# Loads taken apart and moved ahead, and a multiply put off, in a one-core training step of two linear-attention and two gated layers

## The chip, the cores and the metric

The kernel runs on one core of a Trainium2 chip. The metric is the device time of one execution in microseconds (us); smaller is better. The kernel before takes 1132.42 us, the median of three runs (1132.08 to 1135.51 us). The profiled execution, which all lines of the profile below come from, has a span of 1134.6 us.

## The reference

`x` has 2048 rows of 512 bf16 values. Four layers are applied, A, B, A, B, each to the layer norm of `x` and added to `x`; the two A layers share their weights, and so do the two B layers. The kernel returns the output and the gradients of `x` and of all five weights for a given `grad_out`.

```python
def _A_ref(x, wqkv, wo):              # linear attention, 32 heads of 16
    q, k, v = split_heads(x @ wqkv)
    phi = lambda t: jnp.where(t > 0, t + 1, jnp.exp(t)) + 1e-6
    pq, pk = phi(q), phi(k)
    kv = einsum("bhsd,bhse->bhde", pk, v);  z = einsum("bhsd->bhd", pk)
    o = einsum("bhqd,bhde->bhqe", pq, kv) / (einsum("bhqd,bhd->bhq", pq, z)[..., None] + 1e-6)
    return merge_heads(o) @ wo

def _B_ref(x, w_gate, w_up, w_down):  # 512 -> 1376 -> 512
    return (_sigmoid(x @ w_gate) * (x @ w_up)) @ w_down

x = x + _A_ref(_layernorm(x), wqkv, wo);  x = x + _B_ref(_layernorm(x), w_gate, w_up, w_down)
x = x + _A_ref(_layernorm(x), wqkv, wo);  x = x + _B_ref(_layernorm(x), w_gate, w_up, w_down)
# returned: x, and the gradients of sum(x * grad_out)
```

## The kernel before

Rows are handled in 4 blocks of 512 (`NBLK`), a block in 4 tiles of 128 rows, and the 1376 columns of a B layer in 11 chunks `fc` of 128. The layers are numbered 0 to 3. In order of time the program runs: layer 0 (A) to about 74 us, layer 1 (`b_fwd`, with the second half of layer 0 between its chunks) to about 250 us, layer 2 (A), then `b_both`, which does layer 3 forward and backward at once, to about 525 us; then backward through layer 2 (`a_bwd`, to 642 us), layer 1 (`b_bwd`, to 767 us) and layer 0 (`a_bwd`, to about 888 us); and last the weight gradients, the tail, to the end. A scheduler orders the instructions of each engine; each engine then works through its own list. The queue of SyncE (SP) issues most transfers, in the order of its list.

In the code, `...` marks what is cut, and L numbers are the lines that the profile names. The gated chunk, used in `b_fwd` and `b_both`. `hh` is the hidden value, `sd` holds the two factors that the backward pass needs:

```python
def glu(k, hT, fc):
    mm4(k, g_ps[:], ...wg...);  mm4(k, u_ps[:], ...wu...)          # 4 + 4 matmuls
    nc.scalar.activation(g_ps[:], g_ps[:], ACT.Tanh, scale=-0.5)   # L647
    nc.scalar.activation(sd[:, 0, :], g_ps[:], ACT.Identity, bias=k.onef[:], scale=-1.0)           # L648
    nc.vector.scalar_tensor_tensor(hh[:], sd[:, 0, :], 0.5, u_ps[:], ALU.mult, ALU.mult)           # L649
    nc.scalar.activation(sd[:, 1, :], g_ps[:], ACT.Identity, bias=k.onef[:])                       # L650
    nc.gpsimd.tensor_tensor(sd[:, 1, :], sd[:, 1, :], hh[:], ALU.mult)                             # L651
```

In `b_fwd`, `down(b)` multiplies the hidden values by `w_down`, adds to `x`, and asks at once for the layer norm of the next layer (`nxt.need`). In `b_both` each chunk ends with a multiply on VectorE:

```python
            hh, dd = glu(k, ln.hT[b], fc)
            mm4(k, ps[:], ...wdT..., ...gTs...)                    # dhh_ps
            nc.scalar.mul(dhh[:], ps[:], 0.5)                      # L732
            k.last_mul = nc.vector.tensor_tensor(dd, dhh..., dd, ALU.mult)     # L733
```

`k.last_mul` also holds back the transposing loads of the two weights that `b_both`'s own backward half (`dh_b`, L790) needs; a small memset on GpSimd follows the second of them:

```python
def load_b_bwd(k, t, nm, first):
    held(k, first, nc.sync.dma_start_transpose(out=t[:, 0:NFC - 1, :], in_=k.w_in[nm][:, 0:(NFC - 1) * P]))  # L418
    nc.sync.dma_start_transpose(out=t[:, NFC - 1, :], in_=k.w_in[nm][:, F - P:F])                            # L419
    nc.gpsimd.memset(t[0:FDUP, NFC - 1, :], 0.0)                                                             # L420
```

Backward through an A layer, first half. `qr` holds two saved arrays of a block, `qp` and `rp`, and the pool `p_sh` has two buffers:

```python
    for b in range(NBLK):
        qr = k.p_sh.tile([P, 2, NDC, SB], BF16, name="qr_l", tag="sh")
        qp, rp = qr[:, 0], qr[:, 1]
        nc.sync.dma_start(out=flat(qr), in_=sv["qr"][b])                       # L991, 1024 KB
        nc.sync.dma_start(out=flat(qn), in_=sv["qn"][b])
        dqT = p_dq.tile([P, NDC, SB], BF16, name="dqT_t")                      # 4 buffers
        for dc in range(NDC):
            mm4(k, ps[:], ...MT..., ...gT...)                                  # dq_ps
            k.mark = nc.scalar.copy(dq[:], ps[:])                              # L1005, dq_sb, 3 buffers
            nc.vector.tensor_tensor(u_t[:], dq[:], qp[:, dc, :], ALU.mult)     # L1007
            # two steps later, soft():
            nc.tensor.matmul(t_ps[:], lhsT=k.bdmask[:], rhs=u_t[:], ...)       # L977
            nc.vector.scalar_tensor_tensor(w_t[:], t_ps[:], nz, dq[:], ...)    # L979
            nc.gpsimd.tensor_tensor(dqT[:, dc, :], w_t[:], rp[:, dc, :], ALU.mult)   # L980
            nc.vector.scalar_tensor_tensor(u_t[:], t_ps[:], -1.0, qp[:, dc, :], ...) # L981
```

The tail. A gradient of 512 columns takes one pass over 16 row tiles for each of two layers; `pieces` loads the turned operand by transposing transfers into the pool `dw_set_end` (6 buffers of 512 rows), `load_all` the row operand (2 MB), and `put` takes a finished bank out of PSUM:

```python
        k.p_set, k.p_dst = pool("dw_set_end", 6), pool("dw_stage_end", 6)
        for i, a in ((0, 1), (1, 0), (1, 1), (2, 0), (2, 1)):
            if (i, a) == (2, 0):
                g1 = load_all(...)                 # into a pool of its own
            joint(i, a)                            # w_up, w_gate: L1199
        for i, s in enumerate(SETS):
            dw_rows(k, "wd", s, [(g1, sv[1]["hhT"])], sv[3]["wd"])     # w_down: L1217
            if i == 0:   h2 = load_all(...)
            elif i == 1: h0 = load_all(...)
        for i, nm in ((1, "dkT"), (0, "dqT")):     # w_qkv: L1199
            dw_cols(...)
            if i: dw_small(k)                      # L1148, L1153

def put(...):  k.nc.scalar.copy(new[0:r, 0:w], ps);  ...dma_start(out=..., in_=new)     # L1126
```

Of the kernel before, what the change touches and what calls it, by code (L numbers as in the profile page):

```python
# [16 lines left out]
D = 512  # L17
# [3 lines left out]
P = 128  # L21
# [612 lines left out]

def glu(k, hT, fc):

    nc = k.nc
    g_ps = k.ps.tile([P, SB], F32, name="g_ps", tag="bank")
    mm4(k, g_ps[:], lambda c: k.wg[:, c, FC0[fc]:FC0[fc] + P], lambda c: hT[:, :, c, :])
    u_ps = k.ps.tile([P, SB], F32, name="u_ps", tag="bank")  # L640
    mm4(k, u_ps[:], lambda c: k.wu[:, c, FC0[fc]:FC0[fc] + P], lambda c: hT[:, :, c, :])
    hh = k.p_hh.tile([P, SB], BF16, name="hh_t")
    if k.n_sd % 2 == 0:
        k.sd2 = k.p_sd.tile([P, 2, 2, SB], BF16, name="sd_t", tag="sd")
    sd = k.sd2[:, k.n_sd % 2]
    k.n_sd += 1
    nc.scalar.activation(g_ps[:], g_ps[:], ACT.Tanh, scale=-0.5)  # L647
    nc.scalar.activation(sd[:, 0, :], g_ps[:], ACT.Identity, bias=k.onef[:], scale=-1.0)  # L648
    nc.vector.scalar_tensor_tensor(hh[:], sd[:, 0, :], 0.5, u_ps[:], ALU.mult, ALU.mult)  # L649
    nc.scalar.activation(sd[:, 1, :], g_ps[:], ACT.Identity, bias=k.onef[:])  # L650
    nc.gpsimd.tensor_tensor(sd[:, 1, :], sd[:, 1, :], hh[:], ALU.mult)  # L651
    return hh, sd
# [7 lines left out]
def b_fwd(k, l, ln, nxt):  # L660
# [9 lines left out]
    def down(b):  # L670
        ys = [k.ps.tile([P, D], F32, name="y_ps", tag="bank") for _ in range(NB)]
        for fcs in (range(NFC - 1), (NFC - 1,)):
            for j in range(NB):
                for fc in fcs:
                    nc.tensor.matmul(ys[j][:], lhsT=hhs[b][fc][:, rows(j)], rhs=k.wd[:, fc, :],
                                     start=(fc == 0), stop=(fc == NFC - 1))
        for j in range(NB):
            add_x(k, b * NB + j, ys[j])
        nxt.need(b * NB + NB - 1)

    for b in range(NBLK):
# [3 lines left out]
        for fc in range(NFC):  # L685
            hh, sd = glu(k, ln.hT[b], fc)
            hhs[b].append(hh)
            if late:
                store()
            late.append((b, fc, hh, sd))  # L690
            yield b, fc
    store()
    down(NBLK - 1)


# [8 lines left out]
def b_both(k, l, ln, ctx):  # L704
# [6 lines left out]
    def down(b):  # L711
        for j in range(NB):
# [6 lines left out]
            if j % 2:  # L719
                k.st.dma_start(out=by_tile(k.out0, st - 1, 2), in_=ost[:])  # L720

    for b in range(NBLK):
        ln.need(b * NB + NB - 1)
# [3 lines left out]
        for fc in range(NFC):  # L727
# [4 lines left out]
            nc.scalar.mul(dhh[:], ps[:], 0.5)  # L732
            k.last_mul = nc.vector.tensor_tensor(dd, dhh[:].unsqueeze(1).to_broadcast([P, 2, SB]), dd, ALU.mult)  # L733
            hhs[b].append(hh)
            dds[b].append(dd)
            if b:
                turn_dd(k, sv, b, fc, dd)
            else:
                store_dd(k, sv, b, fc, dd, nc.sync)
            store_hh(k, sv, b, fc, hh, k.st)  # L740
# [7 lines left out]
            if b == NBLK - 1 and fc == 5:  # L748
                k.early = a_grads(k, 0)
            yield b, fc  # L750
    b = NBLK - 1
    down(b)
# [45 lines left out]
def backward(k):  # L798
    nc, tc = k.nc, k.tc
    with ExitStack() as ctx:  # L800
# [19 lines left out]
        k.fill.step(NFC * NST)  # L820
        h3, h1 = load_all(k, sv[3]["h"], "h_all"), load_all(k, sv[1]["h"], "h_all")
        joint = lambda i, a: dw_cols(k, ("wu", "wg")[a], 0, SETS[i],
                                     [(h3, sv[3]["ddT"][a], sv[3]["ddN"][:, :, :, a]), (h1, sv[1]["ddT"][a])])
        k.p_dst = mpool("dw_stage", 6)
        joint(0, 0)
        mctx.close()
        k.p_set, k.p_dst = pool("dw_set_end", 6), pool("dw_stage_end", 6)
        k.p_sm = pool("dw_small", 2)
        p_all, p_end = k.p_all, pool("dw_all_end", 2)
        for i, a in ((0, 1), (1, 0), (1, 1), (2, 0), (2, 1)):  # L830
            if (i, a) == (2, 0):
                k.p_all = p_end
                g1 = load_all(k, sv[1]["g"], "g_all")
                k.p_all = p_all
            joint(i, a)
        for i, s in enumerate(SETS):
            dw_rows(k, "wd", s, [(g1, sv[1]["hhT"])], sv[3]["wd"])
            if i == 0:
                h2 = load_all(k, sv[2]["h"], "h_all")
            elif i == 1:  # L840
                h0 = load_all(k, sv[0]["h"], "h_all")
        for i, nm in ((1, "dkT"), (0, "dqT")):
# [118 lines left out]
def a_bwd1(k, l, big, ph1, p_dq):  # L961
# [4 lines left out]
    CT_ps = [k.ps2.tile([P, D], F32, name="CT_ps", tag="dwbank") for _ in range(NDC)]  # L966
    late, gs, dqTs = [], [k.early], []

# [5 lines left out]

    def soft(b, dc, dq, u_t, qp, rp, dqT):
        t_ps = k.ps.tile([P, SB], F32, name="t_ps", tag="bank")
        nc.tensor.matmul(t_ps[:], lhsT=k.bdmask[:], rhs=u_t[:], start=True, stop=True)  # L977
        w_t = ph1.tile([P, SB], BF16, name="w_t")
        nc.vector.scalar_tensor_tensor(w_t[:], t_ps[:], A["nz"][:, dc:dc + 1], dq[:], ALU.mult, ALU.add)  # L979
        nc.gpsimd.tensor_tensor(dqT[:, dc, :], w_t[:], rp[:, dc, :], ALU.mult)  # L980
        nc.vector.scalar_tensor_tensor(u_t[:], t_ps[:], -1.0, qp[:, dc, :], ALU.mult, ALU.mult,  # L981
                                       accum_out=dzp[:, dc, b:b + 1])
        if dc == NDC - 1:
            k.st.dma_start(out=by_chunk(sv["dqT"], b), in_=dqT[:])

    k.fill.step(12)
    for b in range(NBLK):
        g_t, gT = gs[b]
        qr = k.p_sh.tile([P, 2, NDC, SB], BF16, name="qr_l", tag="sh")
        qp, rp = qr[:, 0], qr[:, 1]  # L990
        nc.sync.dma_start(out=flat(qr), in_=sv["qr"][b])  # L991
        qn = k.p_h.tile([P, NDC, NB, P], BF16, name="qn_l", tag="h_t")
        nc.sync.dma_start(out=flat(qn), in_=sv["qn"][b])
        if b == 1 and l == 2:
            nc.sync.dma_start_transpose(out=k.woT[:], in_=k.w_in["wo"])
            nc.sync.dma_start_transpose(out=k.wqkvT[:], in_=k.w_in["wqkv"])
        if b == NBLK - 1 and l == 2:
            held(k, k.mark, nc.sync.dma_start_transpose(out=k.wdT[:], in_=k.w_in["wd"]))
        dqT = p_dq.tile([P, NDC, SB], BF16, name="dqT_t")
        dqTs.append(dqT)  # L1000
        for dc in range(NDC):
# [5 lines left out]
            nc.vector.tensor_tensor(u_t[:], dq[:], qp[:, dc, :], ALU.mult)  # L1007
            late.append((b, dc, dq, u_t, qp, rp, dqT))
            k.fill.step(2)
            if len(late) > 2:  # L1010
                soft(*late.pop(0))
            if dc in (0, 2) and b + 1 < NBLK:
                g = a_grads(k, b + 1, dc // 2)
                if dc:
                    gs.append(g)
        sums(b, g_t, qn)
    while late:
# [104 lines left out]
def put(k, ps, nm, rs, cs, eng=None):  # L1122

    r, w = ps.shape[0], ps.shape[1]
    new = k.p_dst.tile([P, D], BF16, name="dw_new")
    k.nc.scalar.copy(new[0:r, 0:w], ps)  # L1126
    (eng or k.st).dma_start(out=k.outs[nm][rs, cs], in_=new[0:r, 0:w])  # L1127
# [29 lines left out]

def load_all(k, src, name):
    t = k.p_all.tile([P, NST, D], BF16, name=name, tag="all")
    for b in range(NBLK):  # L1160
        k.nc.sync.dma_start(out=t[:, b * NB:(b + 1) * NB, :], in_=by_tile(src, b * NB, NB))
    return t


def pieces(k, nat, src, c0, w, turned=None):

    for b in range(NBLK):
        if len(nat.shape) == 2:
            n = k.p_set.tile([P, NB, D], BF16, name="nat_t", tag="set_t")
            k.nc.sync.dma_start(out=n[:], in_=by_tile(nat, b * NB, NB))  # L1170
        t = k.p_set.tile([P, NB, w], BF16, name="set_t", tag="set_t")
# [4 lines left out]
        for j in range(NB):  # L1176
            st = b * NB + j
            yield st, (n[:, j, :] if len(nat.shape) == 2 else nat[:, st, :]), t[:, j, :]

# [75 lines left out]
```

## Time and profile before

| What | Value |
|---|---|
| Time, median of three runs | 1132.42 us |
| Span of the profiled execution | 1134.6 us |
| TensorE (PE) busy | 1074.8 us |
| VectorE (DVE) busy | 529.1 us |
| ScalarE (ACT) busy | 487.7 us |
| GpSimd (POOL) busy | 324.5 us |
| Moved by DMA | 248.12 MB, 219 GB/s in the mean |

How to read it: the busy times say how full an engine is over the whole span, not what it waited for. The list of waits names, for each engine, the line that stood idle and whose end released it, with the total, the number of times and the longest. The view by stretches of time gives the busy time of each engine in a stretch, the clock that TensorE was granted (1.00 is full), and the share of the 16 DMA engines in use (it can come out a little above 1). The timeline lists instructions in order, with the idle time before each in brackets. A matmul of 512 columns is shown as 379 ns long, but they overlap: the timeline has 11 of them starting every 2.37 us, so one occupies TensorE for 0.216 us.

### The profile page before, as it was taken

How to read it: one execution, taken by the hardware profiler on the slowest of the kernel's cores; microseconds unless marked ns; L12 is line 12 of the kernel's file. 1: busy time of each engine (PE TensorE's matmuls, PEld its weight loads, DVE VectorE, ACT ScalarE, POOL GpSimd, SP SyncE). 2: the span in 40 equal slices, each digit the busy share in tenths (PEclk: the TensorE clock that was granted, in tenths of full speed). 3: DMA queues.
4: the chain of work that ended last, by engine and by line, in shares of the span. 5: the costliest groups of instructions: out<-in, count | busy, mean ns of one | idle time of the engine just before them, and what ended most of it. 6: DMA issues, size and time to landing. Idle time of an engine off the chain costs nothing.

```text
span 1134.6 us, 15573 instructions
## 1 busy us (share of the span) xinstructions
PE 1074.8 (95%) x5529; PEld 509.6 (45%) x5624; DVE 529.1 (47%) x983; ACT 487.7 (43%) x1002; POOL 324.5 (29%) x427
## 2 busy tenths in 40 slices
PE   6989999998899999999899999999799999999898
PEld 3444444444334444444444444444344444464343
DVE  7685765667734445434657634546667100000100
ACT  3476977547635546453434533336236200000011
POOL 5425645303632625141433200003523200001110
PEclk9999999999999999999999999999999999999999
DMA  8977888679993939399996798759982797699995
GB/s 260 263 229 241 249 244 242 192 180 240 281 231 84 251 81 247 80 253 274 221 342 163 218 274 235 230 186 285 322 223 85 177 280 176 149 179 238 276 232 134
DMA packets 376557, 248.12 MB, mean 219 GB/s; under 512 B 288784, under 2 KB 341040, under 8 KB 374688
## 3 DMA queue, kind: packets, MB, share of 16 engines
q1 hardware_dynamic: 361424, 197.73, 70.0%
q0 software_dynamic: 15056, 49.39, 13.1%
q8 instruction: 44, 0.72, 0.3%
q14 instruction: 33, 0.27, 0.1%
HBM read 74.48 MB, written 102.20 MB: 156 GB/s over the span
## 4 chain that ended last, share of the span: by engine, by line
PE 26%; issue 20%; POOL 4%; DMA 3%; DVE 2%; ACT 1%; POOLq 0%; SPq 0%; DVEq 0%; ACTq 0%
PE dh_ps L885 7%; PE dhh_ps L180 3%; PE fill_ps L236 3%; DMA qr_l<-sv_qr 2%; PE dw_ps L1199 2%; PE dh_ps L790 2%; PE dq_ps L180 2%; PE dh_ps L1107 2%; PE CT_ps L972 2%; PE dh_ps L1046 1%; POOL out_dram L1127 1%; PE dpk_ps L180 1%; POOL x L865 1%; PE y_ps L180 1%; POOL out_dram L1224 1%
## 5 line engine op out<-in xcount | busy, mean ns | idle before, releaser
L1199 PE MATMUL dw_ps<-set_t,h_all 128*128 128x512 bf16 (+1 forms) x1008 | 203.9, 362 | 2.5 <-ACT dw_new L1126 1.7
L1199 PEld LDWEIGHTS <-h_all 128*128 128x128 bf16 x1024 | 100.1, 98 | 105.7 <-issue 2.2
L651 POOL TENSOR_TENSOR sd_t<-sd_t,hh_t 128x512 bf16<-128x512 bf16 x88 | 105.5, 1208 | 120.0 <-DVE hh_t L649 89.2
L1126 ACT CAST dw_new<-dw_ps 128x512 bf16<-128x512 f32 (+1 forms) x40 | 19.8, 573 | 220.6 <-PE dw_ps L1199 156.6
L855 ACT ACTIVATE t_sb<-dh_ps,rstd 128x512 f32<-128x512 f32 x64 | 43.5, 680 | 133.3 <-PE dh_ps L790 94.8
L180 PE MATMUL g_ps<-hT_t,wg 128*128 128x512 bf16 x352 | 90.5, 379 | 7.3 <-DVE hh_t L649 4.0
L1223 DVE TENSOR_TENSOR dw_new<-dw_ps,part_l 128x512 bf16<-128x512 f32 (+1 forms) x11 | 7.2, 689 | 181.7 <-PE dw_ps L1217 154.8
L180 PE MATMUL u_ps<-hT_t,wu 128*128 128x512 bf16 x352 | 90.5, 379 | 0.6 <-DVE hh_t L649 0.6
L180 PE MATMUL dhh_ps<-gT_t,wdT 128*128 128x512 bf16 x341 | 89.3, 379 | 0.5
L649 DVE SCALAR_TENSOR_TENSOR hh_t<-sd_t,u_ps 128x512 bf16<-128x512 bf16 x88 | 59.3, 679 | 14.0 <-ACT sd_t L648 13.5
L885 PE MATMUL dh_ps<-wuT,dd_t 128*128 128x512 bf16 x173 | 65.6, 379 | 0.2
L885 PE MATMUL dh_ps<-wgT,dd_t 128*128 128x512 bf16 x170 | 64.4, 379 | 0.2
L1127 POOL DMA_DIRECT2D out_dram<-dw_new x36 | 19.2, 541 | 150.8 <-ACT dw_new L1126 149.3
L648 ACT ACTIVATE sd_t<-g_ps,onef 128x512 bf16<-128x512 f32 x88 | 60.8, 691 | 2.5
L650 ACT ACTIVATE sd_t<-g_ps,onef 128x512 bf16<-128x512 f32 x88 | 60.6, 688 | 0.0
L733 DVE TENSOR_TENSOR sd_t<-dhh_t,sd_t 128x1024 bf16<-128x1024 bf16 x44 | 30.4, 692 | 61.1 <-POOL sd_t L651 59.8
L908 DVE TENSOR_TENSOR dd_t<-dhh_t,sh_t 128x1024 bf16<-128x1024 bf16 x44 | 29.9, 690 | 58.7 <-ACT dhh_t L906 48.1
L647 ACT ACTIVATE g_ps<-g_ps 128x512 f32<-128x512 f32 x88 | 52.4, 602 | 8.8 <-PE g_ps L180 8.7
L180 PEld LDWEIGHTS <-wg 128*128 128x128 bf16 x352 | 33.9, 98 | 47.0 <-issue 8.8
L180 PEld LDWEIGHTS <-wu 128*128 128x128 bf16 x352 | 34.4, 98 | 42.3 <-issue 0.9
L790 PEld LDWEIGHTS <-sd_t 128*128 128x128 bf16 x352 | 34.5, 98 | 41.5
L885 PEld LDWEIGHTS <-dd_t 128*128 128x128 bf16 x352 | 34.4, 98 | 41.5
(172 smaller groups left out, 1857.8 us busy)
## 6 DMA issues: line engine op xcount, KB each, us to landing
sv_sd<-sd_t SPq DMA_DIRECT2D x44, 256.0 KB, 2.9
sv_ddT<-dd_t SPq DMA_DIRECT2D x40, 256.0 KB, 4.3
sv_h<-h_t POOLq DMA_DIRECT2D x16, 512.0 KB, 5.4
sv_qr<-pe_t POOLq DMA_DIRECT2D x16, 512.0 KB, 5.7
qr_l<-sv_qr SPq DMA_DIRECT2D x8, 1024.0 KB, 7.6
sh_t<-sv_sd SPq DMA_DIRECT2D x8, 1024.0 KB, 7.2
h_all<-sv_h SPq DMA_DIRECT2D x16, 512.0 KB, 6.0
sv_ddN<-nat_t SPq DMA_DIRECT2D x6, 1024.0 KB, 4.4
```

Of the source, the lines that this page charges most:

```text
L180: i = k.nc.tensor.matmul(out, lhsT=lhs(c), rhs=rhs(c), start=(c == 0), stop=(c == n - 1))
L236: nc.tensor.matmul(ps[0:w, :], lhsT=t[:, st, 0:w], rhs=self.g[st // NB][:, st % NB, :], start=(st == 0), stop=(st == NST - 1))
L647: nc.scalar.activation(g_ps[:], g_ps[:], ACT.Tanh, scale=-0.5)
L648: nc.scalar.activation(sd[:, 0, :], g_ps[:], ACT.Identity, bias=k.onef[:], scale=-1.0)
L649: nc.vector.scalar_tensor_tensor(hh[:], sd[:, 0, :], 0.5, u_ps[:], ALU.mult, ALU.mult)
L650: nc.scalar.activation(sd[:, 1, :], g_ps[:], ACT.Identity, bias=k.onef[:])
L651: nc.gpsimd.tensor_tensor(sd[:, 1, :], sd[:, 1, :], hh[:], ALU.mult)
L790: k.nc.tensor.matmul(dh_ps[:], lhsT=dds[fc][:, a, rows(j)], rhs=(k.wuT, k.wgT)[a][:, fc, :], start=(i == 0), stop=(i == 2 * NFC - 1))
L855: nc.scalar.activation(t_sb[:], dh_ps, ACT.Identity, scale=rstd, accum_out=c1[:])
L885: nc.tensor.matmul(acc[b][j][:], lhsT=dd[:, a, rows(j)], rhs=(k.wuT, k.wgT)[a][:, fc, :], start=(fc == 0 and a == 0), stop=(fc == NFC - 1 ...
L1127: (eng or k.st).dma_start(out=k.outs[nm][rs, cs], in_=new[0:r, 0:w])
L1199: k.nc.tensor.matmul(ps[ic][:, 0:w], lhsT=h_m[:, ic * P:(ic + 1) * P], rhs=t_m, start=(m == 0), stop=(m == n - 1))
```

## The change

The change has several parts, all meant to take away waits without altering what is computed:

- In `b_fwd`, every second chunk forms the second factor `(tanh + 1) * hh` in one VectorE instruction straight from PSUM, where it took one on ScalarE and one on GpSimd. The layer norm of the next layer is asked for later, in two portions.
- In `b_both`, the VectorE multiply of a chunk (`scale`) is issued one chunk later.
- In the backward pass of an A layer, `qr` is loaded as two halves. `qp` of two blocks shares one buffer of `p_sh`; the other half goes straight into `dqT`, which GpSimd then multiplies in place. The loads are asked for a block ahead.
- In the tail, the row operands `g1` and `h2` go into buffers that the activations of the backward pass leave free (`p_h`, `p_hT`), and all three are asked for earlier; the freed space gives nine buffers for the turned operand instead of six, and ten for results; `put` alternates between VectorE and ScalarE.

```diff
-def glu(k, hT, fc):
+def glu(k, hT, fc, fused=False):
@@
-    nc.scalar.activation(sd[:, 1, :], g_ps[:], ACT.Identity, bias=k.onef[:])
-    nc.gpsimd.tensor_tensor(sd[:, 1, :], sd[:, 1, :], hh[:], ALU.mult)
+    if fused:
+        nc.vector.scalar_tensor_tensor(sd[:, 1, :], g_ps[:], 1.0, hh[:], ALU.add, ALU.mult)
+    else:
+        nc.scalar.activation(sd[:, 1, :], g_ps[:], ACT.Identity, bias=k.onef[:])
+        nc.gpsimd.tensor_tensor(sd[:, 1, :], sd[:, 1, :], hh[:], ALU.mult)
@@ b_fwd
-        nxt.need(b * NB + NB - 1)
@@
-            hh, sd = glu(k, ln.hT[b], fc)
+            hh, sd = glu(k, ln.hT[b], fc, fc % 2 == 1)
@@
+            if b and fc in (2, 4):
+                nxt.need((b - 1) * NB + (1 if fc == 2 else 3))
@@
     down(NBLK - 1)
+    nxt.need(NST - 1)
@@ b_both
+    def scale(b, fc, dhh, dd):
+        k.last_mul = nc.vector.tensor_tensor(dd, dhh..., dd, ALU.mult)
+        ...                                  # turn_dd or store_dd, as before
@@
-            k.last_mul = nc.vector.tensor_tensor(dd, dhh..., dd, ALU.mult)
+            if late:
+                scale(*late.pop())
+            late.append((b, fc, dhh, dd))
@@ backward
-        k.p_set, k.p_dst = pool("dw_set_end", 6), pool("dw_stage_end", 6)
+        k.p_set, k.p_dst = pool("dw_set_end", 9), pool("dw_stage_end", 10)
@@
-            if (i, a) == (2, 0):
-                ...
-                g1 = load_all(k, sv[1]["g"], "g_all")
+            if (i, a) == (1, 0):
+                g1 = load_all(k, sv[1]["g"], k.p_h, "h_t")
+            elif (i, a) == (2, 0):
+                h2 = load_all(k, sv[2]["h"], k.p_hT, "hT_t")
@@
             if i == 0:
-                h2 = load_all(k, sv[2]["h"], "h_all")
-            elif i == 1:
-                h0 = load_all(k, sv[0]["h"], "h_all")
+                h0 = load_all(k, sv[0]["h"], k.p_all, "all")
@@ a_bwd1
+    def loads(b):
+        if b % 2 == 0:
+            qps.append(k.p_sh.tile([P, 2, NDC, SB], BF16, name="qp_l", tag="sh"))
+        dqTs.append(p_dq.tile([P, NDC, SB], BF16, name="dqT_t"))
+        nc.sync.dma_start(out=flat(qps[-1][:, b % 2]), in_=sv["qr"][b][:, 0:half])
+        nc.sync.dma_start(out=flat(dqTs[b]), in_=sv["qr"][b][:, half:2 * half])
+        qns.append(k.p_h.tile([P, NDC, NB, P], BF16, name="qn_l", tag="h_t"))
+        nc.sync.dma_start(out=flat(qns[b]), in_=sv["qn"][b])
@@
-        nc.gpsimd.tensor_tensor(dqT[:, dc, :], w_t[:], rp[:, dc, :], ALU.mult)
+        nc.gpsimd.tensor_tensor(dqT[:, dc, :], w_t[:], dqT[:, dc, :], ALU.mult)
@@
-        qr = k.p_sh.tile([P, 2, NDC, SB], BF16, name="qr_l", tag="sh")
-        ...
+        qp, dqT, qn = qps[b // 2][:, b % 2], dqTs[b], qns[b]
@@
                 if dc:
                     gs.append(g)
+                    loads(b + 1)
@@ put
-    k.nc.scalar.copy(new[0:r, 0:w], ps)
+    k.n_put += 1
+    (k.nc.vector.tensor_copy if k.n_put % 2 else k.nc.scalar.copy)(new[0:r, 0:w], ps)
@@ pieces
-        if len(nat.shape) == 2:
-            ...                              # a branch that no caller used
```

## The prediction

> **What bounds the kernel now.** I read the page's busy times first, then the waits of TensorE, then the stretches around each wait, then the other engines there.
>
> ```profile
> PE 1074.8 (95%) x5529; PEld 509.6 (45%) x5624; DVE 529.1 (47%) x983; ACT 487.7 (43%) x1002; POOL 324.5 (29%) x427
> ```
>
> TensorE is the bound: 59.8 us of the 1134.6 us span are not busy. Of these 5.9 us lie before the first matmul and 3.4 us after the last (the chain ends it at 1131.2 us); the change touches neither. So about 50 us of holes can be filled, 4.5% of the time, and no matmul is removed. The waits of TensorE (total us, times, longest) say who makes the holes:
>
> ```profile
> PE dq_ps L180 <- ACT dq_sb L1005: 6.5, 2, 3.5
> PE T_ps L285 <- DVE h_t L281: 5.9, 1, 5.9
> PE y_ps L180 <- DVE pe_t L535: 5.3, 4, 2.6
> PE dw_ps L1217 <- DMA set_t<-sv_hhT: 4.2, 1, 4.2
> ...
> PE t_ps L977 <- DVE u_t L981: 3.2, 1, 3.2
> PE y_ps L180 <- DVE hh_t L649: 2.6, 1, 2.6
> ...
> PE dw_ps L1199 <- ACT dw_new L1126: 1.7, 2, 1.2
> ```
>
> Lines 1 and 5 are the A-layer backward passes (563, 795 and 808 us), lines 3 and 6 mostly block 0 of `b_both`, lines 4 and 7 the tail. A hole can also cost after it has ended. The stretches just behind three of them:
>
> ```profile
> 325.00:330.00 5.00, 4.53 (x14) 1.77 (x15) 2.34 (x5) 2.81 (x5) 3.34 (x4) 0.67 1.23 268
> ...
> 566.00:571.00 5.00, 4.49 (x14) 1.66 (x14) 3.66 (x10) 1.04 (x2) 4.30 (x4) 0.66 1.26 205
> ...
> 1059.00:1064.00 5.00, 5.00 (x17) 2.17 (x16) 0.00 (x0) 0.00 (x0) 0.00 (x0) 0.68 1.14 217
> ```
>
> The third number from the right is the granted clock. A mean of 0.67 over 5 us costs 5 x 0.33 = 1.65 us, so each of these holes costs 1.6 to 1.7 us more than the list of waits shows, about 5 us in all. The two holes at 795 and 808 us are followed by a clock of 1.00.
>
> [...] here L651 takes 1208 ns on GpSimd and L649 679 ns on VectorE, 1.8 times. [...]
>
> **The change, part by part.**
>
> *A-layer backward.* The view of the tile `qr_l` has VectorE waiting for this load:
>
> ```profile
>   DMA qr_l<-sv_qr: 13.8, 3
> ```
>
> Blocks 2 and 3 cannot load until block 0 or 1 has left one of the two buffers; then 1024 KB take 8 to 10 us on the chain. VectorE stops, `dq_sb` (3 buffers) is not freed, ScalarE stops, and TensorE has no bank. In the compiled order of the changed program all four `qp` halves are issued before the pass begins, with no wait for a block's use; the other halves go to four buffers of their own. The holes are 3.5 us + 1.7 us of clock at 563 us, and 3.2 + 3.0 us in layer 0: 11.4 us. Against it: in layer 2 the first `dqT` half now stands behind the two transposing weight loads, whose issue ends at 533.8 us, and GpSimd wants it at 534.1 us. GpSimd starts perhaps 5 us late, but each step has some 2.7 us for 1.2 us of its work, so it catches up. I expect **-9.5 us**.
>
> *Tail.* DMA is full there and the transposed tiles arrive late:
>
> ```profile
> 1060.00:1075.00 15.00, 14.95 (x65) 6.93 (x65) 2.04 (x3) 0.00 (x0) 1.61 (x3) 0.93 1.18 224
> ```
>
> A transposing load takes about 3.0 us (four in 12.05 us of SP's queue at 1050 us), and TensorE uses it up in 16 x 0.216 = 3.45 us, so DMA is barely ahead, and a 2 MB row load in the queue puts it behind. The change moves `h2` and `g1` (4 MB) to before the tail, where DMA is slack (share 0.25 at 851 to 879 us), leaving one 2 MB load in this place, and nine buffers instead of six give 3 x 3.45 = 10 us more lead. I expect the hole of 4.2 us and its 1.65 us of clock to go. The 1.7 us behind `put` come from 12 evictions in a row on ScalarE, about 0.52 us each, against 3.5 us of matmuls in `dw_small`; two engines halve that, so most of it goes. Together **-6.5 us** of 7.5.
>
> *`b_fwd`.* 20 chunks (5 of 11, 4 blocks) lose 0.69 us on ScalarE (13.8 us) and 1.21 us on GpSimd (24 us) and gain 0.68 us on VectorE (13.6 us). TensorE's holes there are 1.3 us twice, 1.0, 0.5 and 0.3 us, 4.4 us together, most of them waiting for `hh_t` on VectorE just after `down`, when four adds and four layer-norm writes stand ahead of it. Putting the layer norm off clears that; the fused instruction adds VectorE time (112 of 177 us busy, 126 after) and holds the bank of `g_ps` longer. **-3 us**.
>
> *`b_both`.* Putting the multiply off lets VectorE run past GpSimd. The holes in block 0 (to 325 us) are 7.7 us, plus 1.65 us of clock. But here I expect a new wait. The timelines of GpSimd, VectorE and SP:
>
> ```profile
> 321.15 0.51 POOL L420 MEMSET wuT<- 32x512 bf16 x1 [7.35 <-PE g_ps L180]
> ```
>
> ```profile
> 324.08 0.69 DVE L733 TENSOR_TENSOR sd_t<-dhh_t,sd_t 128x1024 bf16<-128x1024 bf16 x1 [7.95 <-POOL sd_t L651]
> ```
>
> ```profile
> 318.41 1.17 SPq L419 DMA_TRANSPOSE wuT<-in_B_w_up_dram  x1
> ...
> 321.56 5.82 SPq L418 DMA_TRANSPOSE wuT<-in_B_w_up_dram  x1
> 327.43 6.83 SPq L418 DMA_TRANSPOSE wgT<-in_B_w_gate_dram  x1
> ```
>
> Before, the two short weight loads went first and the memset ran 2.7 us later; it blocked GpSimd, VectorE and so TensorE. In the changed order the long load L418 stands ahead of each short one, so the memsets come some 8 and 16 us later; GpSimd runs them after the multiplies of chunk 10 and of the next block's chunk 1. The `wgT` load still lands about 19 us after the buffers come free at 318.4 us (327.43 + some 10). TensorE first wants `wgT` at 338.7 us now, hardly later. If it comes faster to that point, it waits there, unless the buffers come free earlier too. So of 9.4 us I count **-4**, and -0.5 for the rest of `b_both`.
>
> *Sum.* 9.5 + 6.5 + 3 + 4 + 0.5 = 23.5 us. Against it I set 4 us for holes that appear where none are now, since TensorE has nothing to spare after each stage. 1132.4 - 19.5 is about **1113 us**.
>
> **The rivals.**
> 1. *The `b_both` gain is lost or turned over to `wgT`.* For it speaks the changed order and a DMA share of 1.0 to 1.1 from 255 to 340 us. Then 3 to 6 us less: about 1118 us.
> 2. *VectorE becomes the bound of `b_fwd`.* For it: it gains 13.6 us and holds two banks longer. Against it: in the fullest slice (113 to 142 us) it is at 20.2 of 29 us, while ScalarE is at 26.2. If so, that stage loses 3 us: about 1119 us.
> 3. *The tail stays DMA-bound.* For it: share above 1.1 from 1045 to 1105 us, the bytes unchanged, and `h0` now where `h2` was. Then the hole only moves: about 1119 us.
> 4. *All holes named go, with their slow clock.* 11.4 + 7.5 + 4.4 + 9.4 + 1.7 = 34.4 us: about 1098 us. The `wgT` wait speaks against it.
>
> **Range and chances.** One rival true costs about 5 us, two some 10: the top is 1122 us. The bottom, 1104 us, lies halfway between my undiscounted sum (1109 us) and rival 4. 2% faster is 1109.8 us, which needs 22.6 us, nearly all of my undiscounted sum: 0.3. Slower by 2% would need a hole of over 40 us: 0.01.
>
> **What would show it.** After: no wait of VectorE for `qp_l` and no clock of 0.66 near 566 us; no TensorE wait on `set_t<-sv_hhT`; TensorE busy nearly unchanged at 1075 us, the span down by as much as the holes. In `b_both`, the first `wgT` matmul waiting for L418 or for the memset, and GpSimd's memset behind a wait of 8 us or more. The prediction is wrong if GpSimd's late start in layer 2 reaches TensorE through `w_t` (2 buffers), or if SP's list stalls ahead of the tail on a buffer that is freed late.

## The result, and the profile after

The changed kernel takes **1116.68 us** (median of 4 runs, 1115.05 to 1122.19) against 1132.25 us for the kernel before, run beside it: a ratio of 0.987, 95% interval [0.983, 0.991], some 15.6 us less. A second series gave 0.983 [0.980, 0.986], 19.4 us less. It is faster, and by less than 2% at the middle of the first interval.

The profiled run of it has a span of 1120.5 us, the slowest of its four. The first line of its page, the busy time of each engine:

```profile
PE 1077.4 (96%) x5624; PEld 509.1 (45%) x5624; DVE 551.5 (49%) x1023; ACT 468.1 (42%) x962; POOL 303.6 (27%) x407
```

TensorE's busy time is what it was (1074.8 us before), so what was won are holes: 43.1 us are not busy instead of 59.8 us. Some 5 us of that difference are no holes won: the profile before lacks 95 of the 5624 matmul records, and each leaves a gap of 0.05 us (two matmuls start 2 x 0.216 us apart around it, and one is shown as 0.379 us long). So the 50 us of holes that the prediction saw to fill were some 45 us. The waits of TensorE (total us, times, longest us) show which ones went and which came:

```profile
PE y_ps L180 <- DVE pe_t L535: 3.1, 4, 1.9
PE dh_ps L802 <- DMA wgT<-in_B_w_gate_dram: 2.6, 1, 2.6
PE dpk_ps L180 <- DMA haT_l<-sv_hT: 2.3, 1, 2.3
...
PE t_ps L997 <- DVE u_t L1001: 2.1, 1, 2.1
...
PE fill_ps L236 <- DVE dkT_t L1075: 1.9, 1, 1.9
...
PE g_ps L180 <- DVE hh_t L649: 1.1, 2, 0.7
...
PE dq_ps L180 <- ACT dq_sb L1020: 0.3, 2, 0.2
```

Line 7 was 6.5 us, lines 1 and 6 were 5.3 and 4.0 us, and the two waits of the tail (4.2 and 1.7 us) are gone from the list. Lines 2, 3 and 5 are new: a hole each where none stood in the profile before. Line 4 has moved: in the profile before it was the hole at 795 us in layer 0 behind `qr_l`, now it lies at 539 us in layer 2 and ends with another tile. The clock behind three holes and where the old one stood, and a stretch of the tail (busy time of each engine, then clock, DMA share, GB/s):

```profile
331.00:335.00 4.00, 3.29 (x9) 1.18 (x9) 1.99 (x4) 0.00 (x0) 1.97 (x3) 0.57 1.08 287
539.00:544.00 5.00, 5.00 (x23) 2.33 (x22) 3.38 (x8) 1.66 (x3) 3.27 (x4) 0.66 1.01 256
566.00:571.00 5.00, 5.00 (x37) 2.75 (x35) 4.39 (x8) 1.95 (x4) 2.88 (x3) 1.00 1.12 363
832.00:837.00 5.00, 5.00 (x17) 1.87 (x16) 3.50 (x8) 0.08 (x1) 0.00 (x0) 0.66 0.31 122
1060.00:1075.00 15.00, 15.00 (x71) 6.80 (x70) 0.84 (x2) 0.00 (x0) 1.43 (x3) 1.00 1.15 240
```

At 566 us the clock is full now, but 0.66 stands at 539 and 832 us instead: 1.7 us each. The slow stretch of the first line, behind the wait for `wgT`, stands where the profile before had one at 325 us. In the tail TensorE is busy all the time and DMA is nearly as full as it was (1.15, from 1.18).

What makes the new holes is read from the timelines (start us, us, engine, line, tiles, then in brackets the idle time before and what ended it). First GpSimd in layer 2, then SP and TensorE in layer 0:

```profile
535.49 3.56 POOL L1000 TENSOR_TENSOR dqT_t<-w_t,dqT_t 128x512 bf16<-128x512 bf16 x3 [7.72 <-DMA dqT_t<-sv_qr]
```

```profile
814.13 12.79 SPq L1194 DMA_TRANSPOSE set_t<-sv_ddT  x2
827.01 0.53 SPq L1051 DMA_DIRECT2D haT_l<-sv_hT  x1
```

```profile
831.84 4.67 PE L180 MATMUL dpk_ps<-haT_l,Wp_t 128*128 128x512 bf16 x13 [2.31 <-DMA haT_l<-sv_hT]
```

GpSimd stands 7.72 us for the first `dqT` half, which is behind the two transposing weight loads. VectorE's list of waits has what follows from it:

```profile
DVE w_t L999 <- POOL dqT_t L1000: 5.7, 2, 5.3
```

It stands 5.3 us for one of the two `w_t` buffers, and so TensorE stops 2.13 us for `u_t`. In layer 0 two transposing loads for the tail hold SP's list for 12.79 us, `haT_l` is issued behind them at 827 us, and TensorE waits for it.

By program stage, from the first matmul of each stage in the two profiles (us). The spread is the matmul into `rd_ps`, in the second half of an A layer; the tail counts from its own first matmul, which lies at 877.6 us before:

| stage | before | after | difference |
|---|---|---|---|
| to the first `glu` of `b_fwd` | 77.7 | 77.1 | -0.6 |
| `b_fwd`, to layer 2's first spread | 174.0 | 171.3 | -2.8 |
| from there into `b_both`, to the first `wuT` matmul | 84.6 | 78.2 | -6.4 |
| `b_both`, the rest | 189.3 | 193.8 | +4.5 |
| A-layer backward, layer 2 | 116.2 | 116.7 | +0.5 |
| `b_bwd` | 127.7 | 127.6 | -0.1 |
| A-layer backward, layer 0 | 108.1 | 106.8 | -1.3 |
| tail | 253.7 | 245.6 | -8.1 |

The tail and `b_fwd` behave as the prediction has it. `b_both` wins and hands much of it back: of the 4.5 us, 2.6 are the wait for `wgT` and 1.4 the slow clock behind it. The A-layer stages, the largest item of the prediction, win next to nothing. The experiments ask whether that is so outside of this one execution, and why.

### The profile page after: what moved, and what is told of

Same layout as the page of the kernel before. It is cut to its first block, busy times and chain, and to the rows that moved or that the text cites. A ratio compares the mean times of both kernels' runs of the same rounds, so it can differ in the third digit from the quotient of the medians.

```text
span 1120.5 us, 15624 instructions
## 1 busy us (share of the span) xinstructions
PE 1077.4 (96%) x5624; PEld 509.1 (45%) x5624; DVE 551.5 (49%) x1023; ACT 468.1 (42%) x962; POOL 303.6 (27%) x407
## 4 chain that ended last, share of the span: by engine, by line
PE 51%; DMA 2%; DVE 1%; ACT 1%; SPq 0%; issue 0%; POOL 0%; ACTq 0%; DVEq 0%
PE dw_ps L1217 18%; PE dh_ps L894 7%; PE dh_ps L1123 3%; PE dw_ps L1235 3%; PE dhh_ps L180 3%; PE fill_ps L236 3%; PE dh_ps L1062 2%; PE CT_ps L992 2%; PE dpk_ps L180 2%; PE dq_ps L180 2%; PE dh_ps L802 2%; PE y_ps L180 1%; DMA hf_t<-sv_hhT 1%; PE t_ps L997 1%; DMA pkT_l<-sv_pkT 1%; DMA dqT_t<-sv_qr 1%
## 5 line engine op out<-in xcount | busy, mean ns | idle before, releaser
L1217 PE MATMUL dw_ps<-set_t,rows_t 128*128 128x512 bf16 (+1 forms) x1024 | 204.4, 362 | 0.0
L1217 PEld LDWEIGHTS <-rows_t 128*128 128x128 bf16 x1024 | 100.2, 98 | 103.6
L654 POOL TENSOR_TENSOR sd_t<-sd_t,hh_t 128x512 bf16<-128x512 bf16 x68 | 83.7, 1231 | 155.3 <-DVE hh_t L649 111.9
L1143 DVE CAST dw_new<-dw_ps 128x512 bf16<-128x512 f32 (+1 forms) x20 | 12.4, 653 | 185.7 <-PE dw_ps L1217 184.6
L1143 ACT CAST dw_new<-dw_ps 128x512 bf16<-128x512 f32 (+1 forms) x20 | 10.5, 562 | 222.5 <-PE dw_ps L1217 201.6
L894 PE MATMUL dh_ps<-wgT,dd_t 128*128 128x512 bf16 x176 | 66.7, 379 | 0.0
L648 ACT ACTIVATE sd_t<-g_ps,onef 128x512 bf16<-128x512 f32 x88 | 60.4, 690 | 2.8
L647 ACT ACTIVATE g_ps<-g_ps 128x512 f32<-128x512 f32 x88 | 52.4, 598 | 11.2 <-PE g_ps L180 10.9
L180 PEld LDWEIGHTS <-wdT 128*128 128x128 bf16 x352 | 34.4, 98 | 41.3
```

The lines of the kernel that those rows point to most:

```text
L180: i = k.nc.tensor.matmul(out, lhsT=lhs(c), rhs=rhs(c), start=(c == 0), stop=(c == n - 1))
L894: nc.tensor.matmul(acc[b][j][:], lhsT=dd[:, a, rows(j)], rhs=(k.wuT, k.wgT)[a][:, fc, :], start=(fc == 0 and a == 0), stop=(fc == NFC - 1 ...
L1217: k.nc.tensor.matmul(ps[ic][:, 0:w], lhsT=h_m[:, ic * P:(ic + 1) * P], rhs=t_m, start=(m == 0), stop=(m == n - 1))
```

## The experiments

### One part at a time

The first four kernels are the kernel before with one part of the change each; the kernel before took 1136.58 us beside them.

**The tail alone**: row loads into freed activation tiles, nine operand and ten eviction buffers, evictions on two engines.

```
-        k.p_set, k.p_dst = pool("dw_set_end", 6), pool("dw_stage_end", 6)
+        k.p_set, k.p_dst = pool("dw_set_end", 9), pool("dw_stage_end", 10)
...
+            if (i, a) == (1, 0):
+                g1 = load_all(k, sv[1]["g"], k.p_h, "h_t")
...
+    (k.nc.vector.tensor_copy if k.n_put % 2 else k.nc.scalar.copy)(new[0:r, 0:w], ps)
```

> The kernel before with the tail's part of the change alone (earlier row loads into freed buffers, nine slots, ten result buffers, put on two engines). Theory of the prediction: the 4.2 us wait for set_t<-sv_hhT, the slow clock behind it and most of the 1.7 us behind put go, and nothing else changes: 6.5 us faster than the kernel before, about 1126 us. Rival (the tail stays bound by DMA): the hole only moves, 0 to 2 us faster. Third possibility, from the trace of the changed kernel: the early row loads crowd SP's list ahead of the tail and open a hole of 2 to 4 us near 830 us, so that only 3 us remain.

Measured: 1128.80 us, ratio 0.9932 [0.9914, 0.9950], 7.7 us less. Its tail takes 245.61 us, to the hundredth what the changed kernel's takes. The feared hole near 830 us is there with 0.5 us.

**The split query loads alone**.

```
-        nc.sync.dma_start(out=flat(qr), in_=sv["qr"][b])
+        nc.sync.dma_start(out=flat(qps[-1][:, b % 2]), in_=sv["qr"][b][:, 0:half])
+        nc.sync.dma_start(out=flat(dqTs[b]), in_=sv["qr"][b][:, half:2 * half])
```

> The kernel before with the split, earlier loads of the A-layer backward passes alone. Theory: the waits for qr_l (3.5, 3.2 and 3.0 us) and one slow-clock window of 1.7 us go, 11.4 us, but the late first dqT half gives back 2.1 us and a slow-clock window of 1.7 us in layer 2, as the changed kernel's trace shows: 7 to 8 us faster, about 1125 us, and a wait of t_ps near 540 us. Rival (the late half is an accident of that one execution): 10 to 11 us faster and no such wait.

Measured: 1134.84 us, ratio 0.9993 [0.9974, 1.0013]: between 3 us less and 1.5 us more, where 7 to 8 us less were foretold. Two waits of TensorE that it brought or kept:

```profile
PE dpk_ps L180 <- DMA haT_l<-sv_hT: 2.2, 1, 2.2
PE fill_ps L236 <- DVE dkT_t L1066: 2.1, 1, 2.1
```

`dq_ps` hardly waits for `dq_sb` any more (the hole at 563 us is 0.2 us), as meant. But the waits for `haT_l` and `dkT_t`, and one of 1.8 us at `t_ps` in layer 2, are those of the changed kernel, so they belong to this stage and do not come from the other parts.

**`b_fwd` alone** (fused instruction in five of eleven chunks, layer norm put off), and **the put-off multiply of `b_both` alone**.

```
+        nc.vector.scalar_tensor_tensor(sd[:, 1, :], g_ps[:], 1.0, hh[:], ALU.add, ALU.mult)
...
+            if b and fc in (2, 4):
+                nxt.need((b - 1) * NB + (1 if fc == 2 else 3))
```

> The kernel before with the fused factor in every second chunk of b_fwd and the later layer-norm requests alone. Theory: the two 1.3 us waits for hh_t after down and the 1.0 us wait go: 3 us faster, about 1129 us, visible by 250 us of the trace and kept to the end. Rival (later stages are bound by loads at fixed places): the 3 us are there at 250 us and lost again by 345 us, so 0 to 1 us faster.

```
+            if late:
+                scale(*late.pop())
+            late.append((b, fc, dhh, dd))
```

> The kernel before with the multiply of b_both put off by a chunk alone. Theory of the prediction: the 2.6 us holes of block 0 shrink, the first wgT matmul then waits for its load, which stands behind the long wuT load: 3 to 4 us faster, about 1129 us, with a wait of dh_ps for wgT of 1 to 3 us. Rival: the wgT wait and the slow clock behind it eat the whole gain, 0 to 1 us faster.

Measured: 1133.84 us, ratio 0.9976 [0.9952, 1.0000], 2.7 us less; and 1132.26 us, ratio 0.9967 [0.9950, 0.9984], 3.7 us less, with a wait for `wgT` of 1.6 us, as foretold. Which of the two edits of `b_fwd` did it was not tried apart. The four parts sum to 14.9 us, the whole is worth 15.6 us beside the first runs and 19.4 us in the second series: within the intervals they add up.

These kernels also give three more profiles with the old query loads. The holes of the old loads are not the same twice: at `dq_ps` and `t_ps` they come to 9.7 us in the profile before, with the tail alone to 4.2 us. But then another hole stands in the same stage. The waits of TensorE of the kernel with the tail alone:

```profile
PE fill_ps L236 <- DVE dkT_t L1056: 2.9, 1, 2.9
...
PE dq_ps L180 <- ACT dq_sb L1002: 1.6, 2, 1.4
```

The first of these is absent from the profile before, but stands in all three of the others (2.9 to 3.1 us). So it is not the split that brings it, and one should compare whole stages over several executions, not single holes. That is the table below, at the end of the section.

### Taking the new waits away

The next four ran together: the changed kernel again, and three edits of it. The kernel before took 1136.99 us beside them.

> The changed kernel itself, once more, on the chip of the three runs that follow, as their yardstick and for a second profile. Theory (the waits for the loads of the A-layer backward passes come and go with the load of the DMA engines): the ratio to the kernel before is again 0.987 to 0.988, but the holes at 520 to 600 us and at 832 us have sizes other than in the first profile (2.1, 1.9 and 2.3 us), by a microsecond or more at one of them at least. Rival (the holes belong to the program, the same at each execution): the same holes, within 0.3 us.

Measured: 1115.87 us, ratio 0.9829 [0.9800, 0.9857]. Its span is 1114.2 us, and its waits:

```profile
PE t_ps L997 <- DVE u_t L1001: 2.5, 1, 2.5
...
PE dpk_ps L180 <- DMA haT_l<-sv_hT: 1.3, 1, 1.3
PE dh_ps L802 <- DMA wgT<-in_B_w_gate_dram: 1.1, 1, 1.1
...
PE fill_ps L236 <- DVE dkT_t L1075: 0.8, 1, 0.8
```

The same four holes as in the first profile, with other sizes: every one that goes back to a DMA transfer differs by 0.4 to 1.5 us, and behind the two smaller ones of 1.3 and 1.1 us the clock stays full (its mean over the execution is 0.998, against 0.995 in the first profile). The waits between two engines (`y_ps` 3.1 us, `g_ps` 1.1 us) are the same to a tenth. The theory of this run holds for the holes; the ratio, foretold as 0.987 to 0.988, was lower.

**All `wuT` matmuls of block 0's `dh_b` first**, into four banks, so that `wgT` is wanted later.

```
+    if b == 0:
+        for j in range(NB):
+            ahead.append(bank())
+            mms(ahead[j], j, 0)          # the wuT matmuls of row tile j
```

> The changed kernel, and dh_b of block 0 does the wuT matmuls of all four row tiles (four banks, 20 matmuls of 0.36 us, 7.2 us) before the first wgT matmul. Theory (TensorE waits 2.6 us for the late wgT load[...], and the loads beneath are not faster for a longer wait): the first wgT matmul comes 5.4 us later in the program, so the hole at 331.7 us is gone, with its slow clock: 3 to 4.3 us less than the changed kernel, ratio to the kernel before about 0.984. Rival (the wgT wait is what it was bound to be: the time won here is lost again behind it, at the next block's evictions or at the next load): 0 to 1 us less.

Measured: 1115.34 us (1113.33 to 1116.39), ratio 0.9800 [0.9775, 0.9825]. The wait for `wgT` is gone from the trace, and the stretch from the first `wuT` matmul to the A-layer backward takes 189.3 us instead of 190.5 us in the run beside it. So these two profiles show 1.2 us, about the whole of that wait in the run beside it. The 3 to 4 us that I expected took the hole of the first profile for its usual size, and my count of the matmuls was wrong: 44 go ahead, not 20, and the first `wgT` matmul comes 9.5 us behind the first `wuT` one. In time it is 0.5 us less between the medians and 3.3 us less between the ratios (0.9829 beside it), whose intervals overlap: the runs do not resolve it.

**`woT` and `wqkvT` held until block 0's last `dq_sb`**, so that the `dqT` halves load first.

```
-            nc.sync.dma_start_transpose(out=k.woT[:], in_=k.w_in["wo"])
+            held(k, k.mark, nc.sync.dma_start_transpose(out=k.woT[:], in_=k.w_in["wo"]),
```

> The changed kernel, and the two transposing weight loads (woT, wqkvT) of layer 2's A-layer backward are held until the last dq_sb eviction of block 0, so that the first dqT half no longer stands behind them. Theory (the late dqT half stops GpSimd, hence w_t, hence VectorE, hence t_ps: a hole of 2.1 us and a slow clock window of 1.7 us at 539 us): the hole goes, 2 to 4 us less than the changed kernel, ratio about 0.984. Rival 1 (other waits of the stage take it up, as the DMA engines have the same bytes to move and pkT comes later still): 0 to 1 us less, and the hole at 595 us grows. Rival 2 (woT now comes too late for the A-gradients): a new wait at dwo or E_ps, slower by some us.

Measured: 1115.26 us (1114.43 to 1123.80), ratio 0.9823 [0.9794, 0.9852]: no gain that the runs resolve. In the trace the hole at 539 us and its slow clock are gone (from 520 to 556 us four `dq_ps` matmuls always take 1.02 to 1.03 us, against 1.91 us behind that hole in the run beside it), and the first half of layer 2 takes 52.1 us instead of 56.0 us. GpSimd begins at 526 us, and no longer waits for the `dqT` half:

```profile
526.32 1.15 POOL L1000 TENSOR_TENSOR dqT_t<-w_t,dqT_t 128x512 bf16<-128x512 bf16 x1 [1.09 <-DVE w_t L999]
```

In all seven profiles with the split loads and these weight loads not held, TensorE waits 1.3 to 3.2 us at `t_ps` in layer 2; in both with them held (here and with all three edits, below) it does not wait there. So the chain (`dqT` half, GpSimd, `w_t`, VectorE, `t_ps`) was the cause of that hole. But the wait for `dkT_t` grew to 1.8 us, from 0.8 us in the run beside it; the second half of the layer and `b_bwd` take 1.0 and 1.2 us more. That is the first rival, for about half of what was won.

**`hf_t` and `set_t` held until the last `dpk_ps` matmul**, so that `haT` and `pkT` go ahead of them.

```
+        if fc == 4:
+            held(self.k, self.k.last_dpk, ld)      # ld: the transposing hf_t load
...
+            if k.hold is not None:
+                held(k, k.hold, ld)                # ld: set_t of the first joint
```

> The changed kernel, and the two kinds of transposing loads that stand ahead of haT and pkT in SP's list (the fifth hf_t load in layer 2, the first set_t loads ahead of the tail) are held until the last dpk_ps matmul has been done, so that haT and pkT of the last blocks go ahead of them. Theory (the transposing loads ahead in the list, 3 to 6 us each, make haT and pkT late): the holes at 595 us (1.9 us) and 832 us (2.3 us, with a slow window of 1.7 us) go: 3 to 5 us less, ratio about 0.983. Rival (haT is late for lack of bandwidth, or the held loads are then late themselves): the hole at 832 us stays, or comes back as a wait for hf_t or set_t; 0 to 1 us less.

Measured: **1112.24 us** (1111.70 to 1114.20, below every run of the changed kernel beside it), ratio 0.9784 [0.9759, 0.9808]. SP's timeline shows the order turned round, and TensorE's waits for `haT_l`, and for `dkT_t` at `fill_ps`, are gone:

```profile
812.86 0.33 SPq L1055 DMA_DIRECT2D haT_l<-sv_hT  x1
816.31 0.33 SPq L1057 DMA_DIRECT2D pkT_l<-sv_pkT  x1
...
840.49 2.15 SPq L1198 DMA_TRANSPOSE set_t<-sv_ddT  x1
```

`haT_l` is issued at 813 us instead of 827 us, and the tail, whose first operands now come later, takes its 245.6 us all the same. The theory holds; the loads that were held are not missed. None of the three profiles with them held has either wait; the seven with the split and the loads not held have 1.3 to 3.6 us for `haT_l` and 0.5 to 2.1 us for `dkT_t`.

### All three edits, the old loads once more, and the tail's two causes

The last four ran together, with 1133.52 us for the kernel before.

> The changed kernel with all three edits at once: the wuT matmuls of block 0's dh_b first, woT and wqkvT held until block 0's last dq eviction, hf_t and set_t held behind haT and pkT. Theory (each edit takes away a wait that nothing else takes up): the two A-layer stages together take 213 to 215 us as with the held loads alone, less about 1 us in layer 2 (first half 52 us instead of 53.2), and the wait for wgT is gone (1 to 2.6 us): span 1106 to 1108 us, ratio to the kernel before 0.975 to 0.977. Rival (the stages between 515 and 865 us are bound by the DMA engines, and a wait removed comes back in the next load): no better than the held loads alone, ratio 0.978, or worse.

Measured: 1109.57 us (1107.12 to 1110.28), ratio 0.9775 [0.9741, 0.9809]. It is the lowest median of this study, but against the kernel before it is no better than the held loads alone, 0.9784. The waits for `wgT` and `t_ps` are gone, and another has come up, at the start of the passes:

```profile
PE fill_ps L238 <- DMA hf_t<-sv_hhT: 3.2, 2, 2.3
```

It was 0.6 us with the held loads alone. It can also come without any of the three edits: it was 2.7 us in the run with six operand buffers (below), whose passes are those of the changed kernel. So it may be chance; whether the rival is at work as well, one execution can't tell.

**The held loads with the old query loads**: `a_bwd1` as in the kernel before, all else as in the run with `hf_t` and `set_t` held.

> The changed kernel with hf_t and set_t held behind haT and pkT, but with the query loads of the kernel before (one 1024 KB load into two buffers, issued block by block). It tells whether the split loads are of use at all, or whether the order of the loads was the whole of it. Theory (split loads win in the first half of the A-layer backward pass, the order of the loads in the second): layer 0's first half takes 52.5 to 56.3 us as in every profile with the old loads (50.4 to 50.9 with the split ones), its second half 51.8 us; so 2 to 5 us slower than the held loads with the split ones, ratio 0.980 to 0.983. Rival (the split is worth nothing, as the experiment with it alone read): ratio 0.978, layer 0's first half below 51 us.

Measured: 1116.47 us (1112.34 to 1120.88), ratio 0.9842 [0.9806, 0.9877]. The holes of the old loads are back, at 558 and 789 us:

```profile
PE t_ps L990 <- DVE u_t L994: 3.4, 1, 3.4
PE dq_ps L180 <- ACT dq_sb L1018: 3.3, 2, 3.2
```

So in this one profile the order of the loads wins 3.3 us in layer 2's second half and loses nearly as much in the two first halves (table below): by the sums of the stages it is worth next to nothing without the split, and the split next to nothing without the order.

**Evictions on ScalarE alone**, with ten buffers:

```
-    (k.nc.vector.tensor_copy if k.n_put % 2 else k.nc.scalar.copy)(new[0:r, 0:w], ps)
+    k.nc.scalar.copy(new[0:r, 0:w], ps)
```

> The changed kernel with all weight-gradient evictions on ScalarE again. It tells what of the tail's gain (253.7 us before, 245.6 us after) came from the two engines. Theory (12 evictions in a row behind dw_small made 1.7 us of hole, and two engines took it away): the last part of the tail takes 29 to 30.5 us instead of 27.8, the rest stays: the tail is 247 to 248 us. Rival (ten eviction buffers alone suffice): the tail stays at 245.6 us.

Measured: 1115.44 us, ratio 0.9827 [0.9788, 0.9865], and a tail of 245.61 us: the rival. The reason is in ScalarE's timeline behind `dw_small`, first of the kernel before, then of this one:

```profile
1101.88 0.59 ACT L1126 CAST dw_new<-dw_ps 128x512 bf16<-128x512 f32 x1 [1.36 <-DMA out_dram<-dw_new]
1103.46 1.56 ACT L1126 CAST dw_new<-dw_ps 128x512 bf16<-128x512 f32 x3 [1.00 <-DMA out_dram<-dw_new]
...
```

```profile
1078.45 5.48 ACT L1143 CAST dw_new<-dw_ps 128x512 bf16<-128x512 f32 x11 [63.85 <-PE dw_ps L1217]
1084.15 0.59 ACT L1143 CAST dw_new<-dw_ps 128x512 bf16<-128x512 f32 x1 [0.21 <-DMA out_dram<-dw_new]
```

Before, ScalarE stopped three times (two are shown), 3.6 us in all, for a store to leave one of six buffers. With ten it stops 0.2 us. Whether a second engine with six buffers would have done as well was not tried.

**Six operand buffers**:

```
-        k.p_set, k.p_dst = pool("dw_set_end", 9), pool("dw_stage_end", 10)
+        k.p_set, k.p_dst = pool("dw_set_end", 6), pool("dw_stage_end", 10)
```

> The changed kernel with six operand buffers in the tail instead of nine. It tells whether the row loads moved ahead or the nine buffers took away the 4.2 us hole and its slow clock. Theory of the prediction (both count: a transposing load takes 3.0 us against 3.45 us of matmuls, so only three buffers fewer leave no lead against the one 2 MB row load that is left): a wait for set_t of 1 to 3 us comes back in the part that begins with the down weight, 39 to 42 us instead of 38.0. Rival (moving the row loads ahead was enough): 38.0 us, no wait.

Measured: 1114.54 to 1122.92 us in three executions (a fourth, of 5140.51 us, is left out), ratio 0.9869 [0.9819, 0.9920]. The part that begins with the down weight takes 37.98 us, as with nine: the row loads moved ahead took the hole of 4.2 us away without the three further buffers. But one wait came up in the last part, for 1.4 us of the tail (247.04 us):

```profile
PE dw_ps L1217 <- DMA set_t<-sv_dqT: 1.3, 1, 1.3
```

The rest of the time above the changed kernel's lies outside of the tail, where this kernel is the same program: the holes at 333 and 831 us were 3.0 and 3.6 us in its profile.

### The A-layer backward passes in all profiles

First half: from the pass's first matmul to the first `dpk_ps`; second half: from there to the next stage's first matmul. Times in us, means where there are several profiles.

| query loads, order | profiles | layer 2, first | second | layer 0, first | second | sum |
|---|---|---|---|---|---|---|
| old | 4 | 54.5 | 62.4 | 54.0 | 52.0 | 222.9 |
| split (the change) | 6 | 55.0 | 60.5 | 50.7 | 55.1 | 221.2 |
| split, `woT` held | 1 | 52.1 | 61.0 | 50.9 | 53.8 | 217.8 |
| split, `hf_t`, `set_t` held | 1 | 53.2 | 59.2 | 50.4 | 51.8 | 214.6 |
| split, all three edits | 1 | 53.5 | 59.1 | 50.6 | 51.8 | 215.0 |
| old, `hf_t`, `set_t` held | 1 | 56.2 | 59.1 | 55.1 | 51.8 | 222.2 |

The sums with the old loads lie between 221.5 and 224.3 us, with the split between 220.0 and 223.6 us. The profile of the kernel before, from which the prediction was made, was no odd one as a whole (224.3 us); it had its holes in other places than the rest.

In layer 0 the split does what it was for: 54.0 becomes 50.7 us, and within 0.6 us the same in all nine profiles with it. The second half gives 3.1 us back, as `haT_l` then waits behind the tail's transposing loads. In layer 2 the first half wins nothing, since the `dqT` half stands behind the weight loads. With the order put right the two halves of layer 0 keep what each can have, and the stages take 8 us less than with the old loads.

## Why the prediction was right or wrong

The time lies in the range, 3.7 us above the predicted 1113 us. The steps:

- **A-layer backward, -9.5 us: this step failed.** The split alone brought 0.8 us (-3 to +1.5), and the stages take 1.6 us less over the profiles. That the time still lies in the range is not this step's merit: the other parts brought 14.1 us of the 14 us counted for them, the 4 us set aside made up for less than half of the 8.7 us missing here, and the range had room for the rest. The named holes did go (`dq_ps` behind `dq_sb`: 6.5 to 0.3 us; no clock of 0.66 at 566 us). What failed are two clauses. One: "each step has some 2.7 us for 1.2 us of its work, so it catches up". GpSimd stood 7.72 us for the load, and with two `w_t` buffers VectorE could not go on: a hole of 1.6 to 3.2 us in the six profiles of the split. The text named this among the things that would make it wrong, and gave it no microsecond. Two: the stage was treated as its first half alone. I had not asked what next stands in SP's list behind the loads that became faster; it was `haT_l` and `pkT_l`, behind a transposing load of 6.2 us in layer 2 (7.2 us in the profile before) and two of 12.8 us together in layer 0, there for a later stage.
- **The 4 us set against new holes** were there for just this, and were too few: in the profile after, the three holes of these stages named above are 6.3 us, with 1.7 us of slow clock behind each of two. One of them, the wait for `dkT_t`, is not the split's: three of the four profiles with the old loads have it, larger. The two terms together were -5.5 us and became -1.6 us.
- **Tail, -6.5 us: right in the hole, short in size, wrong in one cause.** Measured -7.7 us (timed) and -8.1 us (trace), all of the 7.5 us that I had counted before the discount; nothing comes back, since the tail is the last stage and now has no hole left. The 4.2 us went by the row loads moved ahead, the buffers beyond six are worth 1.4 us elsewhere. The 1.7 us behind `put` were not ScalarE's speed ("two engines halve that") but six staging buffers waiting for their stores.
- **`b_fwd`, -3 us: right.** -2.7 us timed, -2.8 us in the trace; the stage takes 171.2 to 171.3 us in all ten profiles with this part and 173.2 to 174.0 us in the four without, and the wait of `g_ps` for `hh_t` falls from 4.0 to 1.1 us.
- **`b_both`, -4 us: right, with its mechanism; the -0.5 us for its rest do not show.** Measured -3.7 us for the part alone; there the rest takes 191.1 us, 1.6 us of it the new wait, against 189.3 us in the profile before. The first `wgT` matmul does wait for the load, and GpSimd's memset stands behind it. From GpSimd's timeline in the profile after:

```profile
325.62 0.52 POOL L420 MEMSET wuT<- 32x512 bf16 x1 [10.64 <-DMA wuT<-in_B_w_up_dram]
```

  The idle time of 10.64 us is the wait of 8 us or more that was foretold. To the first `wuT` matmul the stage wins 4.3 to 6.4 us (old 82.5 to 84.6 us in four profiles, new 78.2 us), and 0.9 to 3.0 us of it go into this wait in the profiles of the changed kernel's own order.
- **The rivals.** The first (the gain of `b_both` turned over to `wgT`) is true in part, and was in the sum. The second (VectorE bounds `b_fwd`) and third (the tail stays DMA-bound) are refuted. The fourth (all holes go) is refuted for the A-layer stages, and true for the tail.
- **The clock behind a hole**, 1.65 us each, was counted as a property of the hole. Its length alone does not decide: a hole of 2.13 us brought it in the profile after, one of 3.24 us did not in the profile before. What else does was not shown; see the last section.

## What to carry to other kernels

A load made earlier doesn't end the question; read on down the issuing engine's list, for there its next customers can stand behind something queued in between. Here `haT_l` stood behind 12.79 us of transposing loads for a later stage, and those were the ones to hold back. Compare stages over several profiles, not single holes of one: here the holes that end with a transfer changed place and size from run to run, while the stages' sum kept within 1 to 2% (221.5 to 224.3 us with the old loads). And when the number of buffers and an engine's speed could each explain a wait, look what ended it: here it was a store, and four more buffers did what a second engine was thought to do (3.6 us of stops became 0.2 us).

## What the runs showed of the hardware that I had not expected

**The slow clock after short holes.** All holes of TensorE of 1.5 us and more past 200 us in the first two profiles, with the granted clock of a stretch that begins with the end of the hole or up to 0.8 us beside it (5 us long, 4 us for the one at 329 us):

| profile | hole begins at, us | length, us | stretch, us | clock in it |
|---|---|---|---|---|
| before | 263.21 | 1.65 | 264.9 to 269.9 | 1.00 |
| before | 302.81 | 2.62 | 305.4 to 310.4 | 1.00 |
| before | 322.86 | 2.56 | 325 to 330 | 0.67 |
| before | 562.99 | 3.52 | 566 to 571 | 0.66 |
| before | 794.57 | 3.24 | 797.8 to 802.8 | 1.00 |
| before | 808.35 | 2.97 | 811.3 to 816.3 | 1.00 |
| before | 1054.05 | 4.20 | 1059 to 1064 | 0.68 |
| after | 259.84 | 1.65 | 261.5 to 266.5 | 1.00 |
| after | 297.26 | 1.93 | 299.2 to 304.2 | 1.00 |
| after | 329.14 | 2.57 | 331 to 335 | 0.57 |
| after | 536.56 | 2.13 | 539 to 544 | 0.66 |
| after | 593.46 | 1.85 | 595.3 to 600.3 | 1.00 |
| after | 829.54 | 2.31 | 832 to 837 | 0.66 |

So it is not the length alone that decides: the hole of 2.13 us brings the slow clock, those of 2.62, 2.97 and 3.24 us do not. Nor is it the place in the program: the hole at `t_ps` in layer 2 was 2.49 us in the changed kernel's second profile, and the four `dq_ps` matmuls behind it took 1.91 us instead of 1.03 us; with the evictions on ScalarE, where the program up to the tail is the same, it was 2.5 us, and the mean clock of that whole execution is 1.000. What decides beside the length was not shown by these runs. In an estimate, the 1.7 us of slow clock behind such a hole (a clock of 0.66 over 5 us) are a cost that may or may not come.

**The time that transposing loads hold SP's list.** Two `set_t` loads of 512 KB each, issued ahead of `haT_l`, took 7.3 to 10.1 us of the list in the four profiles with the old query loads and the old order (7.25 us in the first profile before), and 10.9 to 13.3 us in the seven with the split loads and the old order (12.79 us in the first profile after), though they are instructions of the same form; what else moved at that time differs. A single one ahead of them took 3.7 to 6.3 us and 7.7 to 11.6 us (6.26 and 11.59 us in those two profiles). So in that stage one such load ahead of a needed one held the list for 4 to 12 us, more than the 3.0 us that I had read in the tail.
